# Attention scores straight from the transposed keys, with turned sign and interleaved heads, in a fused attention and two-MoE kernel

## The chip, the cores and the metric

The kernel runs on one core of a Trainium2 chip. The metric is the device time of one execution in microseconds (us). Before the change the median of three runs is 1376.65 us (1376.56 to 1377.2).

The engines are named as the profile names them: PE (TensorE, the matrix engine), PEld (its weight loads), DVE (VectorE), ACT (ScalarE), POOL (GpSimd) and SP (SyncE, which issues nearly all DMAs here). Each runs its own instructions in program order; semaphores tie them together.

## The reference

Block attention over q, k and v (2 batches, 8 heads, 768 positions, 64 wide), then a dense mixture of experts whose gates are balanced by eight Sinkhorn rounds, then a routed mixture of experts. What the change touches is the attention scores:

```
scale = 1/sqrt(64); k_sum = max of k over blocks of 32; v_sum = mean of v over blocks of 32
scores_l = scale * q k^T, kept where |i - j| < 16;   scores_s = scale * q k_sum^T + log(32)
a = softmax over [scores_l, scores_s];   out = a [v ; v_sum]
# dense MoE: P = exp(x w_gate - max); 8 times: divide by row sums, then by column sums
#            out = sum over experts of P[:, e] * relu(x w1[e]) w2[e]
```

## The kernel before, in words

**Attention units.** Attention is cut into 16 units (batch, half of the sequence, pair of heads). The 128 partitions hold two heads of 64 channels each (`par` 0 and 1). A unit has six tiles of 64 queries; each sees a window of 96 key columns and the 24 block maxima `ks`. `transposes_k` (L174) turns the keys into `kT`, a strip of 800 columns, and `transposes_q` (L194) turns the queries into `qT`. `windows` (L203) copies the six overlapping key windows on DVE and the block maxima on ACT into one tile `kTw`, 120 columns per query tile. `scores` (L214) then issues per head six float32 matmuls of 64 by 64 by 120 into one PSUM bank (`sc0` for head 0, `sc1` for head 1), and `hh` picks the upper or lower half of the bank's partitions. `maxima` (L238) adds the mask and takes each row's maximum on DVE, and forms `nb`, minus scale times the maximum, in one small DVE instruction per head. `exponents` (L256) runs six Exp on ACT. `normalise` (L268) divides, with the large multiply on POOL. `flip` (L281) transposes the result on PE, and `apply` (L294) multiplies by the values.

**Order of the work.** `STEPS` (L34) lists these steps, each with the unit that it serves relative to the present one and a cost. The costs say where in the unit's share of time a step's pieces fall; a step that yields in its middle is cut there. `merge` (L835) runs the dense MoE as a sequence of pieces (three large matmuls each) and hands out attention pieces between them: after each piece of the first three MoE units it pulls attention until it has reached `goal`. The first four attention units are done before MoE pieces can be mixed in; short runs of `ones` matmuls (`warm`, L315) are put in there. From MoE unit 3 on, `merge` calls two side tasks between pieces: `token_steps` (36 steps of DVE and ACT work that prepares a Strassen form of the tokens) at every second piece and `gate_steps` (the gate logits and the Sinkhorn rounds, 27 steps) at every third. Whatever is left is run at once at unit 7 or 8. A Sinkhorn round is a `row` step on DVE alone, and a `col` step that begins with a PE product of `ones` and `P` (L934) and goes on with five small DVE instructions.

**PSUM.** In the mixed part, transposes and `apply` share three banks in turn, and `sc0` and `sc1` have one bank each.

Of the kernel before, what the change touches and what calls it, by code (L numbers as in the profile page):

```python
# [19 lines left out]
NEG = -1.0e9  # L20


class Attention:
# [7 lines left out]


    LAG = 2
    STEPS = (  # L34
        ("flip", -LAG, 0.65), ("scores", 0, 1.5), ("windows", 1, 0), ("transposes_q", 1, 0.35),
        ("means", -1, 0.2), ("maxima", 0, 0), ("fill_v", -1, 0), ("exponents", 0, 0),
# [3 lines left out]
    def __init__(self, tc, pool, ident, ones, masks, q, k, v, xhi, xlo, psum):  # L40
# [10 lines left out]
        self.kn, self.qn, self.vw, self.vn, self.sv, self.vs = {}, {}, {}, {}, {}, {}  # L51
        self.kT, self.ks, self.qT, self.kTw = {}, {}, {}, {}
        self.an, self.aT, self.sc = {}, {}, [None, None]
# [140 lines left out]
    def transposes_q(self, b, g, hp):  # L194
        nc = self.nc
        qT = self.pool.tile([128, 384], F32, tag="qT", name="qT", bufs=2)
        qn = self.qn.pop((b, g, hp))
        tr = self.psum("tr", [128, 3, 128])
        self.transpose_rows(tr, qn, 0, self.whole(b, g, hp))
        nc.scalar.copy(qT.rearrange("d (p r) -> d r p", r=3), tr)  # L200
        self.qT[b, g, hp] = qT

    def windows(self, b, g, hp):  # L203
        nc = self.nc
# [7 lines left out]
        self.kTw[b, g, hp] = kTw  # L212

    def scores(self, b, g, hp):  # L214

        nc = self.nc
        qT, kTw = self.qT.pop((b, g, hp)), self.kTw.pop((b, g, hp))
        e = self.pool.tile([128, 2, 3, 120], F32, tag="e", name="e", bufs=self.LAG + 1)
        mx, nb, sm = (
            self.pool.tile([128, 6], F32, tag=n, name=n, bufs=self.LAG + 1) for n in ("mx", "nb", "sm")  # L220
        )
        for par in range(2):
            if par:
                yield
            sc = self.psum(f"sc{par}", [128, 3, 120])
            for j in range(3):
                for hh in range(2):
                    t = 2 * j + hh
                    nc.tensor.matmul(
                        sc[64 * hh:64 * hh + 64, j, :],  # L230
                        qT[64 * par:64 * par + 64, 64 * t:64 * t + 64],
                        kTw[64 * par:64 * par + 64, t, :],
                        start=True, stop=True,
                    )
            self.sc[par] = sc
        self.an[b, g, hp] = e, mx, nb, sm

    def maxima(self, b, g, hp):  # L238
        nc = self.nc
        e, mx, nb, sm = self.an[b, g, hp]  # L240
        for par in range(2):
            sc = self.sc[par]
            for j in range(3):
                qt = 3 * g + j
                m = 0 if qt == 0 else (2 if qt == 5 else 1)
                nc.vector.tensor_tensor_reduce(
                    out=e[:, par, j], in0=sc[:, j], in1=self.masks[:, m], scale=1.0,
                    scalar=-3.0e38, op0=ALU.add, op1=ALU.max,
                    accum_out=mx[:, 3 * par + j:3 * par + j + 1],
                )  # L250
            s = slice(3 * par, 3 * par + 3)
            nc.vector.tensor_scalar(
                out=nb[:, s], in0=mx[:, s], scalar1=-self.scale, scalar2=None, op0=ALU.mult
            )

    def exponents(self, b, g, hp):  # L256
        e, _, nb, sm = self.an[b, g, hp]
        for par in range(2):
            if par:
                yield  # L260
            for j in range(3):
                i = 3 * par + j
                self.nc.scalar.activation(
                    out=e[:, par, j], in_=e[:, par, j], func=ACTF.Exp, scale=self.scale,
                    bias=nb[:, i:i + 1], accum_out=sm[:, i:i + 1],
                )

    def normalise(self, b, g, hp):  # L268
        nc = self.nc
        e, _, _, sm = self.an[b, g, hp]  # L270
        rs = self.pool.tile([128, 6], F32, tag="rs", name="rs", bufs=2)
# [49 lines left out]
    def steps(self, fillers):  # L321
# [22 lines left out]
        for _ in self.transposes_k(*U[0]):  # L344
            yield -LAG
        self.windows(*U[0])
        self.transposes_q(*U[0])
# [32 lines left out]
def make_constants(nc, const, attn):  # L380
# [3 lines left out]
    nc.gpsimd.memset(masks, 0.0)  # L384
    neg = 8.0 * NEG
    for hh in range(2):
# [8 lines left out]
        )  # L395
    nc.gpsimd.memset(masks[:, :, 96:120], 8.0 * LOG_BLOCK)
    nc.gpsimd.memset(masks[0:64, 0, 0:16], neg)
# [437 lines left out]
def merge(attn, moe, sides, late):  # L835
# [4 lines left out]
    for u in moe:  # L840
# [795 lines left out]
def kernel(  # L1636
# [55 lines left out]
    with ExitStack() as stacks:  # L1692
# [186 lines left out]
```

## Time and profile before

| | us |
|---|---|
| median of the three runs | 1376.65 |
| the profiled execution | 1374.23 |
| its span in the trace | 1372.4 |
| PE busy | 1337.4 (97%) |
| DVE busy | 743.5 (54%) |
| ACT busy | 454.3 (33%) |
| POOL busy | 104.6 (8%) |

The profiled execution took 1374.23 us, 1.8 us more than the span from its first to its last instruction, and lies 2.4 us below the median of the other runs. Shares of the span hide that stages have different limits. From the first row on, the stages are: attention alone (to about 50 us), attention mixed with the dense MoE (to about 143 us), the dense MoE with the side tasks (to about 207 us), the dense MoE alone, and the routed MoE from about 1170 us.

### The profile page before, as it was taken

Reading aid. Unit: us, or ns where it says so; the run is one execution under the profiler, and the core shown is the slowest. Engines: PE = TensorE matmul, PEld = TensorE weight load, DVE = VectorE, ACT = ScalarE, POOL = GpSimd, SP = SyncE. Lnnn points to the kernel's source line nnn. Section 1 sums busy time; section 2 is a strip of 40 time slices with the busy share of each in tenths; the row PEclk is TensorE's granted clock in tenths of the full one; section 3 lists DMA queues with packets and bytes.
Section 4 is the critical chain, followed back from the end, with each engine's and each line's share of the span. In section 5 each row is a group of like instructions: output and inputs, shape, how many; then the busy total and the mean of one; then the engine's idle time right before and its main releaser. Section 6 shows DMA issues by size and latency. Waiting matters only on the chain. (4 is left out here: it accounts for less than half of the span.)

```text
span 1372.4 us, 21833 instructions
## 1 busy us (share of the span) xinstructions
PE 1337.4 (97%) x8387; PEld 1176.5 (86%) x8387; DVE 743.5 (54%) x1493; ACT 454.3 (33%) x927; POOL 104.6 (8%) x133
## 2 busy tenths in 40 slices
PE   7999989999999999999999999999999999999996
PEld 7778779998898989989988989899899998788874
DVE  7875594455655555656556555555453347514350
ACT  5866221222323223323223232323221214324451
POOL 5341003200000000000000000000000001111110
PEclk9999999999999999999999999999999999999999
DMA  8742110101101010102011111101021127223440
GB/s 187 160 114 48 32 31 12 51 17 46 32 32 31 32 32 31 54 9 61 10 53 30 33 32 32 31 32 40 23 64 31 60 79 255 69 70 132 154 149 23
DMA packets 90452, 82.71 MB, mean 60 GB/s; under 512 B 44639, under 2 KB 66143, under 8 KB 90336
## 3 DMA queue, kind: packets, MB, share of 16 engines
q1 hardware_dynamic: 87696, 73.34, 18.7%
q0 software_dynamic: 2640, 7.87, 1.7%
q8 instruction: 68, 1.11, 0.4%
q14 instruction: 48, 0.39, 0.1%
HBM read 72.53 MB, written 9.44 MB: 60 GB/s over the span
## 5 line engine op out<-in xcount | busy, mean ns | idle before, releaser
L582 PE MATMUL bank<-hi,hhi 128*128 128x512 f32 x720 | 283.6, 394 | 0.0
L582 PE MATMUL bank<-lo,hhi 128*128 128x512 f32 x720 | 282.8, 393 | 0.0
L582 PE MATMUL bank<-hi,hlo 128*128 128x512 f32 x720 | 282.6, 392 | 0.0
L594 DVE SCALAR_TENSOR_TENSOR acc<-bank,P,acc 128x512 f32<-128x512 f32 x168 | 124.6, 748 | 215.5 <-PE bank L582 215.5
L665 ACT ACTIVATE hhi<-t 128x512 fp32r<-128x512 f32 x144 | 91.3, 634 | 342.9 <-DVE t L691 150.8
L645 PE MATMUL bank<-Thi,hi 128*128 128x256 f32 x576 | 163.3, 283 | 0.0
L645 PE MATMUL bank<-Thi,lo 128*128 128x256 f32 x576 | 163.2, 283 | 0.0
L645 PE MATMUL bank<-Tlo,hi 128*128 128x256 f32 x576 | 162.5, 282 | 0.0
L582 PEld LDWEIGHTS bank<-hi,hlo 128*128 128x128 f32 x720 | 135.4, 188 | 29.2
L582 PEld LDWEIGHTS bank<-hi,hhi 128*128 128x128 f32 x720 | 135.5, 188 | 24.9 <-issue 0.5
L582 PEld LDWEIGHTS bank<-lo,hhi 128*128 128x128 f32 x720 | 135.5, 188 | 23.8
L666 DVE SCALAR_TENSOR_TENSOR hlo<-t,hhi 128x512 fp32r<-128x512 f32 x144 | 99.7, 693 | 100.9 <-ACT hhi L665 100.9
L645 PE MATMUL bank<-xlo,hi 128*128 128x256 f32 x432 | 121.2, 281 | 0.0
L645 PE MATMUL bank<-xhi,hi 128*128 128x256 f32 x432 | 121.2, 281 | 0.0
L645 PE MATMUL bank<-xhi,lo 128*128 128x256 f32 x432 | 121.1, 280 | 0.0
L645 PEld LDWEIGHTS bank<-Thi,hi 128*128 128x128 f32 x576 | 108.8, 189 | 7.9 <-DVE t L690 4.1
L645 PEld LDWEIGHTS bank<-Tlo,hi 128*128 128x128 f32 x576 | 109.0, 189 | 3.8
L645 PEld LDWEIGHTS bank<-Thi,lo 128*128 128x128 f32 x576 | 108.7, 189 | 0.0
L476 DVE TENSOR_TENSOR lo<-raw,hi 128x512 fp32r<-128x512 f32 x120 | 84.3, 716 | 0.6 <-issue 0.3
L645 PEld LDWEIGHTS bank<-xhi,lo 128*128 128x128 f32 x432 | 81.6, 189 | 0.0
L645 PEld LDWEIGHTS bank<-xhi,hi 128*128 128x128 f32 x432 | 81.5, 189 | 0.0
L645 PEld LDWEIGHTS bank<-xlo,hi 128*128 128x128 f32 x432 | 81.5, 189 | 0.0
(287 smaller groups left out, 2203.0 us busy)
## 6 DMA issues: line engine op xcount, KB each, us to landing
raw<-in_moe_w_dram SPq DMA_DIRECT2D x128, 256.0 KB, 2.7
raw<-in_moe_w_dram SPq DMA_DIRECT2D x20, 1024.0 KB, 5.9
kn<-in_k_dram SPq DMA_DIRECT2D x8, 384.0 KB, 4.6
qn<-in_q_dram SPq DMA_DIRECT2D x16, 192.0 KB, 3.9
vn<-in_v_dram SPq DMA_DIRECT2D x8, 384.0 KB, 4.8
x2e<-acc SPq DMA_DIRECT2D x9, 256.0 KB, 2.0
x2d<-acc SPq DMA_DIRECT2D x9, 256.0 KB, 2.3
vw<-in_v_dram SPq DMA_DIRECT2D x16, 96.0 KB, 2.5
```

The costliest lines, as they stand in the source:

```text
L476: self.nc.vector.tensor_tensor(out=lo, in0=src, in1=hi.bitcast(F32), op=ALU.subtract)
L582: nc.tensor.matmul(ps, h, w, start=(n == 0), stop=(n == last))
L594: nc.vector.scalar_tensor_tensor(out=a, in0=ps, scalar=self.P[:, i, e:e + 1], in1=a, op0=ALU.mult, op1=ALU.add)
L645: nc.tensor.matmul(bank[:, 256 * f:256 * f + 256], a[:, o:o + 128], m[:, k], start=first and n == 1, stop=n == 12, skip_group_check=True,)
L665: nc.scalar.activation(out=hi, in_=src, func=ACTF.Relu)
L666: nc.vector.scalar_tensor_tensor(out=lo, in0=src, scalar=0.0, in1=hi.bitcast(F32), op0=ALU.max, op1=ALU.subtract)
```

## The change

The windows are no longer copied: the score matmuls read `kT` and `ks` in place, so each 120-column matmul becomes one of 96 and one of 24 columns. The two heads' matmuls alternate, and all of a unit's scores are issued in one piece. `qT` is scaled by minus the scale when it leaves PSUM; the scores are then negative and scaled, the mask's signs are turned, the row minimum takes the place of the maximum and goes into Exp as its bias, and `nb` falls away. The cost of `scores` in the plan goes from 1.5 to 0.9. In `merge`, attention pieces are pulled two at a time, on every second MoE piece. The side tasks are called at every third and fourth piece.

```diff
-        ("flip", -LAG, 0.65), ("scores", 0, 1.5), ("windows", 1, 0), ("transposes_q", 1, 0.35),
+        ("flip", -LAG, 0.65), ("scores", 0, 0.9), ("transposes_q", 1, 0.35),
...
-        nc.scalar.copy(qT.rearrange("d (p r) -> d r p", r=3), tr)
+        nc.scalar.mul(qT.rearrange("d (p r) -> d r p", r=3), tr, -self.scale)
...
-    def windows(self, b, g, hp):
-        kTw = self.pool.tile([128, 6, 120], F32, tag="kTw", name="kTw", bufs=2)
-        a = self.kT[b, hp][:, 384 * g:800]
-        win = bass.AP(a.tensor, a.offset, [list(a.ap[0]), [64, 6], [1, 96]])
-        nc.vector.tensor_copy(kTw[:, :, 0:96], win)
-        nc.scalar.copy(
-            kTw[:, :, 96:120], self.ks[b, hp].unsqueeze(1).to_broadcast([128, 6, 24])
-        )
...
-        for par in range(2):
-            if par:
-                yield
-            sc = self.psum(f"sc{par}", [128, 3, 120])
-            for j in range(3):
+        self.sc = [self.psum(f"sc{par}", [128, 3, 120]) for par in range(2)]
+        for j in range(3):
+            for own in (False, True):
                 for hh in range(2):
-                    t = 2 * j + hh
-                    nc.tensor.matmul(
-                        sc[64 * hh:64 * hh + 64, j, :],
-                        qT[64 * par:64 * par + 64, 64 * t:64 * t + 64],
-                        kTw[64 * par:64 * par + 64, t, :],
-                        start=True, stop=True,
-                    )
+                    for par in range(2):
+                        t = 2 * j + hh
+                        p = slice(64 * par, 64 * par + 64)
+                        c = 384 * g + 64 * t
+                        nc.tensor.matmul(
+                            self.sc[par][64 * hh:64 * hh + 64, j, slice(96, 120) if own else slice(0, 96)],
+                            qT[p, 64 * t:64 * t + 64],
+                            ks[p] if own else kT[p, c:c + 96],
+                            start=True, stop=True,
+                        )
...
-                    scalar=-3.0e38, op0=ALU.add, op1=ALU.max,
+                    scalar=3.0e38, op0=ALU.add, op1=ALU.min,
...
-            nc.vector.tensor_scalar(
-                out=nb[:, s], in0=mx[:, s], scalar1=-self.scale, scalar2=None, op0=ALU.mult
-            )
...
-                    out=e[:, par, j], in_=e[:, par, j], func=ACTF.Exp, scale=self.scale,
-                    bias=nb[:, i:i + 1], accum_out=sm[:, i:i + 1],
+                    out=e[:, par, j], in_=e[:, par, j], func=ACTF.Exp, scale=-1.0,
+                    bias=mx[:, i:i + 1], accum_out=sm[:, i:i + 1],
...
-            goal += min(4, 4 * (piece + 1) / PIECES[u])
+            goal += min(4, 4 * (piece + 2 - piece % 2) / PIECES[u])
...
-        sides = (token_steps(), 2 * NG - 1, 2, 1), (gate_steps(), 2 * NG, 3, 2)
+        sides = (token_steps(), 2 * NG - 1, 3, 1), (gate_steps(), 2 * NG, 4, 2)
```

PE before, one unit of the mixed part: `ident,e` is `flip`, `kTw,qT` the scores of one head, `xhi`/`xlo` a piece of the MoE, `ident,qn` the query transposes.

```order
L290 MATMUL bank_935<-ident,e 120x128 x3
L290 MATMUL bank_940<-ident,e 120x128 x3
L229 MATMUL bank_949<-kTw,qT 64x120 x6
L562 MATMUL bank_956<-xhi_110,hi_504 128x384
L562 MATMUL bank_956<-xlo_112,hi_504 128x384
L562 MATMUL bank_956<-xhi_110,lo_505 128x384
L229 MATMUL bank_960<-kTw,qT 64x120 x6
L562 MATMUL bank_956<-xhi_110,hi_504 128x384
...
L96 MATMUL bank_974<-ident,qn 128x128 x3
```

PE now at the same place; banks 863 and 864 are the two heads'.

```order
L276 MATMUL bank_850<-ident,e 120x128 x3
L276 MATMUL bank_855<-ident,e 120x128 x3
L220 MATMUL bank_863<-kT_126,qT 64x96
L220 MATMUL bank_864<-kT_126,qT 64x96
...
L220 MATMUL bank_863<-ks,qT 64x24
L220 MATMUL bank_864<-ks,qT 64x24
...
L97 MATMUL bank_890<-ident,qn 128x128 x3
L547 MATMUL bank_897<-xhi_110,hi_407 128x384
L547 MATMUL bank_897<-xlo_112,hi_407 128x384
L547 MATMUL bank_897<-xhi_110,lo_408 128x384
L547 MATMUL bank_897<-xhi_110,hi_407 128x384
```

Two score groups of 6 with a MoE piece behind each have become one group of 24, and two MoE pieces stand together behind it.

DVE before, around the maxima of one unit: `sm` and `rs` end the previous unit's softmax, `kTw` is the window copy of the next unit, ISA is mask and maximum, `kT_124` the key copy two units ahead.

```order
L272 TENSOR_SCALAR sm<-sm 128x6
L273 RECIPROCAL rs<-sm 128x6
L208 COPY kTw<-kT_127 128x6x96
L246 ISA e,mx<-bank_831,masks 128x120
L246 ISA mx 128x1
...
L252 TENSOR_SCALAR nb<-mx 128x3
L246 ISA e,mx<-bank_844,masks 128x120
...
L252 TENSOR_SCALAR nb<-mx 128x3
L185 COPY kT_124<-bank_878 128x3x128
```

DVE now at the same place.

```order
L258 TENSOR_SCALAR sm<-sm 128x6
L259 RECIPROCAL rs<-sm 128x6
L236 ISA e,mx<-bank_863,masks 128x120
L236 ISA mx 128x1
...
L236 ISA e,mx<-bank_864,masks 128x120
...
L186 COPY kT_124<-bank_917 128x3x128
```

The window copy and both `nb` are gone; the rest stands in the same order.

PE before, between two Sinkhorn products: `hi,hhi` and the like are the second MoE matmuls.

```order
L934 MATMUL bank_2317<-P,ones 128x96
L562 MATMUL bank_2305<-xhi_110,hi_2134 128x384
...
L582 MATMUL bank_2329<-hi_510,hhi 128x512
...
L562 MATMUL bank_2351<-xhi_110,hi_2189 128x384
...
L934 MATMUL bank_2357<-P,ones 128x96
```

PE now, between two Sinkhorn products.

```order
L919 MATMUL bank_2513<-P,ones 128x96
L547 MATMUL bank_2505<-xhi_110,hi_2173 128x384
...
L567 MATMUL bank_2529<-hi_2465,hhi 128x512
...
L547 MATMUL bank_2551<-xhi_110,hi_2225 128x384
...
L919 MATMUL bank_2560<-P,ones 128x96
```

Between the two products stood 18 MoE matmuls (six pieces), and now stand 24 (eight pieces). On POOL and on SP the order of instructions is the same before and now.

## Rows read from the trace of the kernel before

**Rows 1.** The page's head.

```profile
span 1372.4 us, 21833 instructions
```

**Rows 2.** Stages: length; busy PE, PEld, DVE, ACT, POOL (count); clock; DMA share, GB/s.

```profile
20.10:50.50 30.40, 27.33 (x327) 24.54 (x327) 25.18 (x85) 25.86 (x83) 15.63 (x17) 0.87 0.79 180
50.50:87.00 36.50, 33.06 (x336) 25.74 (x334) 32.06 (x103) 26.01 (x91) 15.36 (x18) 1.00 0.60 133
87.00:143.00 56.00, 56.00 (x530) 45.64 (x530) 31.16 (x133) 33.82 (x112) 12.98 (x15) 1.00 0.26 64
143.00:207.00 64.00, 58.41 (x290) 47.30 (x289) 50.95 (x129) 18.87 (x37) 0.00 (x0) 0.97 0.12 33
207.00:1170.00 963.00, 962.98 (x5855) 869.30 (x5854) 521.45 (x877) 268.43 (x473) 24.16 (x23) 1.00 0.15 45
```

**Rows 3.** Waits of PE, 0 to 50 us: total us, times, longest.

```profile
PE bank L96 <- DMA qn<-in_q_dram: 4.1, 1, 4.1
PE bank L96 <- DVE sm L272: 1.2, 1, 1.2
PE bank L96 <- DVE lo L476: 1.2, 1, 1.2
```

**Rows 4.** Waits of PE, 50 to 240 us.

```profile
PE bank L934 <- DVE P L929: 3.8, 5, 2.0
PE bank L290 <- DVE kT L185: 3.1, 4, 1.8
PE bank L913 <- DVE lg_max L911: 1.5, 1, 1.5
```

**Rows 5.** Timeline of PE in the mixed part: start, length, instruction.

```profile
58.10 0.44 PE L562 MATMUL bank<-xhi,hi 128*128 128x384 f32 x1
58.38 0.34 PE L562 MATMUL bank<-xlo,hi 128*128 128x384 f32 x1
58.55 0.33 PE L562 MATMUL bank<-xhi,lo 128*128 128x384 f32 x1
58.82 0.83 PE L229 MATMUL bank<-kTw,qT 64*64 64x120 f32 x12
59.58 0.44 PE L562 MATMUL bank<-xhi,hi 128*128 128x384 f32 x1
```

**Rows 6.** Timeline of PE in attention alone.

```profile
25.94 1.10 PE L229 MATMUL bank<-kTw,qT 64*64 64x120 f32 x24
26.97 0.55 PE L96 MATMUL bank<-ident,qn 128*128 128x128 f32 x3
...
27.67 0.92 PE L303 MATMUL bank<-aT,vw 120*64 120x64 f32 x24
28.52 2.05 PE L319 MATMUL bank<-ones 128*128 128x128 f32 x16
```

**Rows 7.** Groups on DVE, 0 to 130 us: busy us, mean ns, idle before.

```profile
L246 DVE CUSTOM_DVE_ANT_0 e<-bank,masks 128x120 f32<-128x120 f32 x96 | 21.7, 274 | 0.8 <-PE bank L229 0.8
L208 DVE COPY kTw<-kT 128x576 f32<-128x576 f32 x16 | 14.9, 929 | 0.0
L252 DVE TENSOR_SCALAR nb<-mx 128x3 f32<-128x3 f32 x32 | 8.6, 268 | 1.1
```

**Rows 8.** Timeline of DVE and POOL around two window copies.

```profile
52.86 0.42 DVE L208 COPY kTw<-kT 128x576 f32<-128x576 f32 x1
...
76.21 1.64 DVE L208 COPY kTw<-kT 128x576 f32<-128x576 f32 x1
...
76.01 1.39 POOL L275 TENSOR_TENSOR e<-e,rs 128x720 f32<-128x720 f32 x1 [4.47 <-DVE rs L273]
```

**Rows 9.** Groups on DVE, 55.26 to 79.73 us (three units).

```profile
L208 DVE COPY kTw<-kT 128x576 f32<-128x576 f32 x3 | 3.9, 1294 | 0.0
```

**Rows 10.** Part of the Sinkhorn stretch; columns as in Rows 2.

```profile
169.00:191.67 22.67, 19.56 (x97) 16.51 (x98) 19.90 (x56) 6.91 (x13) 0.00 (x0) 1.00 0.12 38
191.67:195.08 3.41, 3.41 (x11) 2.93 (x11) 3.27 (x10) 1.00 (x2) 0.00 (x0) 0.50 0.43 134
```

More of the change, by code (lines that the diff above doesn't have):

```diff
@@ L51, in __init__ @@
         self.kn, self.qn, self.vw, self.vn, self.sv, self.vs = {}, {}, {}, {}, {}, {}
-        self.kT, self.ks, self.qT, self.kTw = {}, {}, {}, {}
+        self.kT, self.ks, self.qT = {}, {}, {}
         self.an, self.aT, self.sc = {}, {}, [None, None]
@@ L214, in scores @@
     def scores(self, b, g, hp):
         nc = self.nc
-        qT, kTw = self.qT.pop((b, g, hp)), self.kTw.pop((b, g, hp))
+        qT, kT, ks = self.qT.pop((b, g, hp)), self.kT[b, hp], self.ks[b, hp]
         e = self.pool.tile([128, 2, 3, 120], F32, tag="e", name="e", bufs=self.LAG + 1)
-        mx, nb, sm = (
-            self.pool.tile([128, 6], F32, tag=n, name=n, bufs=self.LAG + 1) for n in ("mx", "nb", "sm")
-        )
-        for par in range(2):
-            if par:
-                yield
-            sc = self.psum(f"sc{par}", [128, 3, 120])
-            for j in range(3):
-                for hh in range(2):
-                    t = 2 * j + hh
-                    nc.tensor.matmul(
-                        sc[64 * hh:64 * hh + 64, j, :],
-                        qT[64 * par:64 * par + 64, 64 * t:64 * t + 64],
-                        kTw[64 * par:64 * par + 64, t, :],
-                        start=True, stop=True,
-                    )
-            self.sc[par] = sc
@@ L236, in scores @@
-        self.an[b, g, hp] = e, mx, nb, sm
+        mx, sm = (
+            self.pool.tile([128, 6], F32, tag=n, name=n, bufs=self.LAG + 1) for n in ("mx", "sm")
+        )
+        self.sc = [self.psum(f"sc{par}", [128, 3, 120]) for par in range(2)]
+        for j in range(3):
+            for own in (False, True):
+                for hh in range(2):
+                    for par in range(2):
[8 more added lines that the diff above has]
+                        )
@@ L238, in maxima @@
+        self.an[b, g, hp] = e, mx, sm
     def maxima(self, b, g, hp):
         nc = self.nc
-        e, mx, nb, sm = self.an[b, g, hp]
+        e, mx, sm = self.an[b, g, hp]
         for par in range(2):
@@ L247, in maxima @@
                     out=e[:, par, j], in0=sc[:, j], in1=self.masks[:, m], scale=1.0,
-                    scalar=-3.0e38, op0=ALU.add, op1=ALU.max,
+                    scalar=3.0e38, op0=ALU.add, op1=ALU.min,
                     accum_out=mx[:, 3 * par + j:3 * par + j + 1],
                 )
-            s = slice(3 * par, 3 * par + 3)
-            nc.vector.tensor_scalar(
-                out=nb[:, s], in0=mx[:, s], scalar1=-self.scale, scalar2=None, op0=ALU.mult
-            )
     def exponents(self, b, g, hp):
-        e, _, nb, sm = self.an[b, g, hp]
+        e, mx, sm = self.an[b, g, hp]
         for par in range(2):
@@ L269, in normalise @@
         nc = self.nc
-        e, _, _, sm = self.an[b, g, hp]
+        e, _, sm = self.an[b, g, hp]
         rs = self.pool.tile([128, 6], F32, tag="rs", name="rs", bufs=2)
@@ L345, in steps @@
             yield -LAG
-        self.windows(*U[0])
         self.transposes_q(*U[0])
@@ L384, in make_constants @@
     nc.gpsimd.memset(masks, 0.0)
-    neg = 8.0 * NEG
+    neg = -NEG
     for hh in range(2):
@@ L395, in make_constants @@
         )
-    nc.gpsimd.memset(masks[:, :, 96:120], 8.0 * LOG_BLOCK)
+    nc.gpsimd.memset(masks[:, :, 96:120], -LOG_BLOCK)
     nc.gpsimd.memset(masks[0:64, 0, 0:16], neg)
```

2 lines of the change are left out of this document (removed).

## The prediction

> **What bounds the kernel now.** I read the stages first. In the trace the span is 1372.4 us [rows 1]; PE is busy in nearly all of it, and from 207 to 1170 us it has no gap at all [rows 2]. Nothing there is touched, so what is won before 207 us arrives at the end, unless a stage before it gives it back. Before 207 us four stages differ. In attention alone (20.1 to 50.5 us) PE, DVE and ACT each have idle time and PE's clock is down for part of it: no engine is full, and transfers and waits set the pace. From 50.5 to 87 us PE is busy 33.06 and DVE 32.06 of 36.5 us, two engines nearly full. From 87 to 143 us PE alone is full. From 143 to 207 us PE has gaps while DVE is busy 50.95 of 64 us [rows 2]. Then I read who ended PE's waits: in attention alone query rows that come late by DMA, 4.1 us, and two waits of 1.2 us put down to DVE [rows 3]; later only DVE, 3.1 us for a bank of transposed keys that is not yet copied out, and 3.8 and 1.5 us for the Sinkhorn steps [rows 4]. PE work and DVE lateness are the two prices to set.
>
> **Part 1: the scores on PE, where they are mixed with MoE pieces.** One head's scores take 0.76 us from their start to the next MoE matmul (58.82 to 59.58). Around them a border is paid: the MoE matmul before them lasts 0.27 us (58.55 to 58.82) instead of 0.17 (58.38 to 58.55), and the first one after such a group 0.28 (58.10 to 58.38) instead of 0.17 [rows 5]. One insertion costs 0.76 + 0.10 + 0.11 = 0.97 us, a unit of two heads 1.94.
>
> Now there is one insertion of 24 matmuls. A float32 matmul streams its columns four times in all, and the upper and lower half of a bank run side by side: six matmuls of 120 columns at 2.4 GHz (the granted clock is 1.00 in this stage, rows 2) are six slots of 2 x 2 x 120 / 2.4 = 0.2 us of passes, two matmuls at a time, so 6 x 0.10 = 0.60 us, and the 0.16 us left of 0.76 is start and end. A 96-column slot is then 0.080 us. A 24-column slot would be 0.020 by streaming alone; the nearest row is the 64-column product of the values: 24 records, 12 slots, from 27.67 to 28.52, so (0.85 - 0.16) / 12 = 0.058 us [rows 6]. I take 0.058. The bounds are 0.020 and 0.100 (as long as a 120-column slot).
>
> That two heads run at the same time is shown where both stand next to each other: 25.94 to 26.97 is 1.03 us [rows 6], while 0.16 + 12 x 0.10 = 1.36 would be one after the other. They overlap by 0.33 although the second head is queued behind all of the first. With the heads alternating I take full overlap: 0.16 + 6 x 0.080 + 6 x 0.058 = 0.99 us, with borders 1.20, so a unit saves 0.74 us. The 24-column bounds make it 0.97 and 0.49. No overlap at all gives 0.16 + 12 x 0.138 = 1.82, with borders 2.03, a loss of 0.09 us.
>
> The trace has 230 score records from 50.5 to 143 us, about 19 insertions of 12, or 9.5 units. So 9.5 x 0.74 = **7.0 us**, between -0.9 and 9.2.
>
> The Trainium skill (TensorEngine Tiling, Instruction Overhead) says that each matmul has some 60 cycles of overhead, so that one column costs as much as sixty; this speaks against cutting 120 into 96 and 24. By it a 24-column slot costs what 60 columns do, 0.050 us, and the saving would be 7.5 us; streaming alone would make it 9.2. No run here has shown 24 columns; the 64-column row above is near the rule.
>
> **Part 2: DVE in the mixed part.** Per unit one window copy (0.929 us mean) and two `nb` (0.268 each) go: 1.47 us [rows 7]. In three units from 55.26 to 79.73 us the copies alone take 3.9 us [rows 9]. The stretch from 50.5 to 87 us holds nearly five units: DVE falls from 32.06 to about 25.5, PE from 33.06 to about 29.7 (4.5 x 0.74). PE is then the fuller engine by 4 us, so most of its 3.1 us of waits for the key copies [rows 4] should go. I take **2.3 us**, between 0 and 3.1. ACT loses its copy of the block maxima and is not near full.
>
> The copy's length is not its own: it takes 0.42 us with POOL quiet and 1.64 while POOL's normalising multiply runs (76.01 for 1.39 us) [rows 8]. So one may ask whether the wait merely passes on to the next DVE instruction. What follows it now is the masked minimum out of PSUM, and the masked maxima of before, the same instruction, averaged 274 ns over all 96, POOL busy or not [rows 7]: nothing passes on there.
>
> The Trainium skill (SBUF — State Buffer, SBUF: two separate sides) says that DVE and GpSimd share a port pair as an exclusive lock, which blocks a DVE instruction with two SBUF inputs or in a two-port mode for the whole of the other's instruction. By that rule the wait could pass to the splits of the weights (two SBUF inputs) a little further on. Then only the bare 0.42 of the copy is sure, part 2 shrinks to about 1 us, and the sum by 1.3.
>
> **Part 3: attention alone.** The same DVE and PE work goes there, but the wait of 4.1 us is for query rows on their way, and SP issues the same DMAs in the same order. The two waits of 1.2 us are met by the same instruction, the query transposes, which also wait for their rows; I count them as transfers. Exp can start on its first sixth instead of its first half. I take **0.8 us**; the bounds are -0.5 (a transfer in a new collision) and 3.3 (both waits and 0.9 of ACT's).
>
> **Part 4: the side tasks.** Sinkhorn waits are 3.8 + 1.5 = 5.3 us [rows 4], and after the longest the clock is at half (0.50) for 3.41 us [rows 10], which costs 1.7 us of PE work. PE did nothing for 2.0 us just before that. Together 7.0 us. Now 24 MoE matmuls stand between two products where 18 stood, so the time in which DVE can finish the `col` and `row` chains grows by a third, and the token steps come at two thirds of the rate. From 169 to 191.67 us DVE was busy 19.90 of 22.67 us [rows 10]; with a third more PE work under it (19.56 x 4/3 = 26), it would be busy about 76%. Some stays: the maximum of the logits is reduced and transposed within one step, so PE still meets DVE's backlog there, and four weight splits fall in a bunch somewhere. I leave 1.7 us standing and take **5.3 us**, between 2.5 and 7.0. The clock's loss should go with the long gap. The steps need 36 calls at 9 per unit and 27 at 7 per unit, so both end within units 3 to 6, before they would be run in a bunch at units 7 and 8; that costs nothing.
>
> Two MoE pieces now stand together, which saves some borders against transposes; there the border is small, and I leave it out.
>
> **The sum.** 7.0 + 2.3 + 0.8 + 5.3 = 15.4 us. The profiled execution took 1374.23 us, so it would take 1358.8; the median of the runs lies 2.4 us above it, and 1376.65 - 15.4 = **1361.3 us**.
>
> **Rivals.** *Less is won, because transfers or DVE keep the mixed part's pace* (about 1366). Half of the waits before 87 us are for rows, and a unit there needs seven or eight DMAs, issued one after another by SP. If from 50.5 to 87 us the pace stays, part 2 and half of part 1 (4.5 x 0.74 = 3.3) go, with part 3: 15.4 - 2.3 - 3.3 - 0.8 = 9.0, or 1367.7; if only the port rule holds or the heads overlap by half, 1363 to 1366. Against it: DVE, not DMA, ended every wait after 50 us [rows 4].
>
> *More is won* (about 1355). Short slots cost 0.020 (9.2), the key waits go entirely (3.1), attention alone gives 2.5 and Sinkhorn 6.8: 21.6, so 1355. For it: every stage loses DVE work. Against it: each term would have to be at its good end.
>
> *Slower: changing the row half costs a drain.* The border of about 0.10 us [rows 5] is paid when PE goes between the full array and half of it. If PE paid the like at each of the 23 changes of head within a unit, the scores would take 0.99 + 2.3 us; over 9.5 units that is 22 us more than forecast and in attention alone, where 6.5 units run, some 12 more beyond the slack: 1361.3 + 34 = 1395. It decides from 15.4 / (16 x 23) = 0.042 us per change on. Against it: the overlap of two neighbouring heads, 1.03 against 1.36 us [rows 6].
>
> *No gain:* the heads run one after the other (part 1 at -0.9) and the Sinkhorn waits stay because DVE is still late there: 2.3 + 0.8 + 0.5 - 0.9 = 2.7, so 1374. Against it: rows 6 again, and the third more of cover.
>
> **Chances.** Forecast (1358 to 1364.5) 0.55, less won 0.23, more won 0.14, slower 0.04, no gain 0.04. A run of this kernel cannot tell less than 0.2%, 2.75 us, from no change; so faster 0.92, same 0.04, slower 0.04. The range from 1354.5 to 1369 holds the forecast, nearly all of "less" and about half of "more".
>
> **What would show it.** Right: in the mixed part one group of score records per unit, about 1.0 us from its start to the next instruction, the two heads' records side by side; no window copies; key-copy waits under 1 us; Sinkhorn waits under 2 us and the clock at 1.00 from 169 to 210 us; from there to the end the same length as before. Wrong: score groups of 1.8 us or more; PE waiting for query or key rows between 50 and 87 us; Sinkhorn waits of 4 us or more, or a side task run in a bunch at unit 7; a tail after 1150 us that is longer than before.

## The result

| | median, us | runs, us | ratio to before, 95% interval |
|---|---|---|---|
| before | 1376.61 | 1375.1 to 1377.2 (4) | |
| the changed kernel | 1359.69 | 1358.83 to 1360.33 (4) | 0.9878, 0.9861 to 0.9896 |

The forecast was 1361.3 us, with a range of 1354.5 to 1369.0. The median fell by 16.9 us where 15.4 were expected. Its profiled execution took 1360.04 us against 1374.23, so the profiles account for 14.2.

### The profile page after: what moved, and what is told of

Its sections match the earlier page's. It is cut to its first block, busy times and chain, and to the rows that moved or that the text cites. A ratio compares the mean times of both kernels' runs of the same rounds, so it can differ in the third digit from the quotient of the medians.

```text
span 1358.3 us, 22536 instructions
## 1 busy us (share of the span) xinstructions
PE 1324.5 (98%) x8771; PEld 1174.7 (86%) x8771; DVE 721.7 (53%) x1445; ACT 449.9 (33%) x911; POOL 103.2 (8%) x133
```

## The profile after

The head of the page, to set against [rows 1]:

```profile
span 1358.3 us, 22536 instructions
```

To see where the 14.1 us of span come from, both traces are cut at the same work, not at the same time. The landmarks are the starts of the 1st, 13th and 29th relu that ACT takes from the dense MoE's banks (`hhi` out of `bank`), and the last relu of the routed MoE. The kernel before, columns as in [rows 2]:

```profile
0.00:57.67 57.67, 47.98 (x554) 42.55 (x556) 44.66 (x148) 38.74 (x128) 25.80 (x52) 0.91 0.78 173
57.67:145.74 88.07, 85.10 (x813) 68.28 (x810) 58.53 (x212) 53.18 (x175) 26.73 (x30) 1.00 0.37 85
145.74:230.09 84.35, 78.77 (x392) 66.46 (x391) 57.50 (x146) 20.86 (x42) 9.38 (x6) 0.98 0.09 26
230.09:1347.03 1116.94, 1113.11 (x6578) 989.45 (x6576) 581.53 (x986) 338.60 (x580) 40.73 (x43) 1.00 0.18 56
```

The changed kernel:

```profile
0.00:58.04 58.04, 44.65 (x712) 41.22 (x713) 33.50 (x126) 37.10 (x121) 24.60 (x52) 0.91 0.76 176
58.04:136.88 78.84, 78.25 (x1037) 68.60 (x1036) 46.93 (x185) 51.41 (x167) 25.69 (x30) 1.00 0.40 92
136.88:214.32 77.44, 75.90 (x393) 65.64 (x392) 57.78 (x147) 20.58 (x41) 4.25 (x3) 1.00 0.09 28
214.32:1332.96 1118.64, 1113.22 (x6578) 989.47 (x6576) 582.22 (x986) 337.88 (x580) 46.71 (x47) 1.00 0.17 56
```

Read the lengths line by line. Up to the first relu nothing is won (0.4 us lost), although DVE works 11 us less and PE 3.3 us less there. The mixed part is 9.2 us shorter, the side stretch 6.9, and the rest 1.7 longer. That last loss cannot be put down to the change: no line of that stretch was touched, and in the 14 traces shown here it lasts 1116.9 to 1119.6 us.

Who ended PE's waits, from 0 to 50 us (to set against [rows 3]):

```profile
PE bank L97 <- DMA qn<-in_q_dram: 6.8, 2, 5.4
PE bank L97 <- DVE mx L236: 1.4, 1, 1.4
```

And from 50 to 250 us (against [rows 4]):

```profile
PE bank L97 <- DMA qn<-in_q_dram: 3.4, 1, 3.4
PE bank L919 <- DVE P L914: 1.1, 1, 1.1
PE bank L898 <- DVE lg_max L896: 0.5, 1, 0.5
```

The waits for the key copies (3.1 us) are gone and the Sinkhorn waits fell from 5.3 to 1.6. But query rows, 4.1 us before, now cost 10.2, and one such wait has moved behind 50 us, where there was none. The timeline of PE shows it, and a window over the stretch behind it shows the clock:

```profile
52.27 0.87 PE L97 MATMUL bank<-ident,qn 128*128 128x128 f32 x3 [3.38 <-DMA qn<-in_q_dram]
```

```profile
52.27:58.00 5.73, 5.72 (x47) 5.36 (x48) 2.34 (x3) 4.41 (x15) 0.28 (x2) 0.73 0.78 160
```

The transposes of a later unit's queries wait 3.4 us ahead of the very first MoE piece, and PE goes on at a granted clock of 0.73 (a mean of stretches at its two levels, 0.5 and 1).

One unit's scores on PE (to set against [rows 5]):

```profile
58.59 0.40 PE L220 MATMUL bank<-kT,qT 64*64 64x96 f32 x8
58.80 0.26 PE L220 MATMUL bank<-ks,qT 64*64 64x24 f32 x8
58.89 0.38 PE L220 MATMUL bank<-kT,qT 64*64 64x96 f32 x8
59.08 0.26 PE L220 MATMUL bank<-ks,qT 64*64 64x24 f32 x8
59.17 0.38 PE L220 MATMUL bank<-kT,qT 64*64 64x96 f32 x8
59.37 0.26 PE L220 MATMUL bank<-ks,qT 64*64 64x24 f32 x8
59.56 0.55 PE L97 MATMUL bank<-ident,qn 128*128 128x128 f32 x3
```

58.59 to 59.56 is 0.97 us for both heads; one head alone took 0.76.

On DVE the masked minimum and the weight splits, 0 to 130 us (against [rows 7]):

```profile
L236 DVE CUSTOM_DVE_ANT_0 e<-bank,masks 128x120 f32<-128x120 f32 x96 | 20.6, 277 | 1.6 <-PE bank L220 1.6
L461 DVE TENSOR_TENSOR lo<-raw,hi 128x512 fp32r<-128x512 f32 x8 | 7.6, 970 | 0.5 <-ACT hi L460 0.3
```

and the same splits in the kernel before:

```profile
L476 DVE TENSOR_TENSOR lo<-raw,hi 128x512 fp32r<-128x512 f32 x8 | 8.9, 1128 | 0.5 <-issue 0.3
```

Neither inherited the window copy's long waits: the minimum kept its length (277 ns after, 274 before) and the splits became shorter. That they became shorter is not the missing copy's doing: in the two kernels below that copy again they take 986 and 988 ns.

## The experiments

Each ratio is to runs of the kernel before on the same chip; the first row has the medians of these runs, and the landmarks of the one trace of that kernel. The stages are set side by side at the landmarks above, with the 5th relu added. Between the 5th and the 13th every kernel here has the same MoE matmuls and five units of scores; between the 1st and the 5th, three to four units.

Each kernel has one trace, so it matters how far two traces of the same work differ. Two pairs show it. Up to the 13th relu "side steps alone" runs the same instructions as the kernel before, and "new scores, old pacing" the same as "one piece at a time"; their edits come into force only later. From the 5th to the 13th relu the traces of a pair agree within 0.01 us. The first relu differs by 0.1 us in one pair and by 2.4 in the other. From the 1st to the 5th one pair takes 21.29 us twice, and the other 28.28 and 30.28, where the longer one ran in part at the lower clock:

```profile
57.67:85.95 28.28, 25.31 (x263) 19.82 (x260) 25.31 (x77) 17.84 (x60) 12.78 (x15) 1.00 0.60 135
57.53:87.81 30.28, 27.85 (x261) 22.37 (x258) 25.33 (x77) 17.82 (x61) 13.51 (x16) 0.89 0.59 126
```

So 2.4 us at the first relu, and 2 us in a stretch with waits, can be luck; a few tenths from the 5th to the 13th are not.

| kernel | median, us | ratio to before, 95% interval | 1st relu | 5th | 13th | 29th |
|---|---|---|---|---|---|---|
| before | 1375.96 to 1377.12 | | 57.67 | 85.95 | 145.74 | 230.09 |
| changed | 1359.69 | 0.9878, 0.9861 to 0.9896 | 58.04 | 80.60 | 136.88 | 214.32 |
| side steps alone | 1369.46 | 0.9956, 0.9938 to 0.9974 | 57.53 | 87.81 | 147.60 | 225.02 |
| new scores, old pacing | 1365.09 | 0.9921, 0.9902 to 0.9939 | 58.15 | 79.44 | 135.14 | 219.47 |
| one piece at a time | 1357.33 | 0.9867, 0.9846 to 0.9889 | 55.79 | 77.08 | 132.77 | 210.22 |
| pairs later | 1363.25 | 0.9910, 0.9893 to 0.9927 | 52.83 | 81.99 | 138.51 | 215.99 |
| heads apart | 1364.79 | 0.9914, 0.9901 to 0.9928 | 59.57 | 84.12 | 143.34 | 220.81 |
| wide block maxima | 1364.55 | 0.9912, 0.9895 to 0.9928 | 57.11 | 82.47 | 143.25 | 220.69 |
| copies read | 1356.63 | 0.9854, 0.9837 to 0.9871 | 56.33 | 80.14 | 134.88 | 212.32 |
| copies idle | 1358.81 | 0.9866, 0.9852 to 0.9880 | 59.08 | 83.89 | 139.56 | 217.00 |
| alternation alone | 1368.36 | 0.9937, 0.9924 to 0.9949 | 57.42 | 84.74 | 139.82 | 224.12 |
| value rows later | 1355.46 | 0.9854, 0.9836 to 0.9872 | 54.17 | 75.47 | 131.17 | 208.63 |
| copies for six units | 1352.88 | 0.9826, 0.9814 to 0.9839 | 55.23 | 77.73 | 132.48 | 209.94 |
| value rows by POOL | 1358.47 | 0.9867, 0.9852 to 0.9881 | 53.73 | 74.75 | 130.45 | 207.88 |

### Which part gave what

**Side steps alone.** The kernel before with one line changed.

```diff
-        sides = (token_steps(), 2 * NG - 1, 2, 1), (gate_steps(), 2 * NG, 3, 2)
+        sides = (token_steps(), 2 * NG - 1, 3, 1), (gate_steps(), 2 * NG, 4, 2)
```

> The kernel before with only the side steps spaced as in the changed kernel (every third and fourth MoE piece). Theory: the 7.0 us that the changed kernel gained between the 13th and the 29th relu of the dense MoE (146 to 213 us in the kernel before) come from the spacing alone: 1376.6 - 7.0 = 1369.6 us, with no change before 143 us and Sinkhorn waits of 2 us or less. Rival: the lighter attention work is what freed DVE at the head of that stretch, and the spacing alone gains 4 us or less: 1372.6 us or more, with Sinkhorn waits of 3 us or more left.

Measured: 6.5 us less. From the 13th to the 29th relu it takes 77.42 us (the changed kernel 77.44, before 84.35), and its Sinkhorn waits are those of the changed kernel:

```profile
PE bank L934 <- DVE P L929: 1.1, 1, 1.1
PE bank L913 <- DVE lg_max L911: 0.5, 1, 0.5
```

The gain of that stretch is the spacing's, and independent of the scores.

**New scores, old pacing.** The changed kernel with the goal and the side steps of before.

```diff
-            goal += min(4, 4 * (piece + 2 - piece % 2) / PIECES[u])
+            goal += min(4, 4 * (piece + 1) / PIECES[u])
...
-        sides = (token_steps(), 2 * NG - 1, 3, 1), (gate_steps(), 2 * NG, 4, 2)
+        sides = (token_steps(), 2 * NG - 1, 2, 1), (gate_steps(), 2 * NG, 3, 2)
```

> The new attention (scores in place, heads alternating, turned sign) with the old pacing: one attention piece at a time, side steps at every second and third MoE piece. Theory: the mixed part gains its 9.2 us as in the changed kernel, and the first stages another 2 to 4 because the query transposes no longer run half a unit ahead of their rows; the side stretch gains nothing: 1376.6 - 9.2 - 3 = 1364.4 us, between 1362 and 1368. Rival: standing MoE pieces together (fewer borders) is a good part of the gain of the mixed part: 1370 us or more.

Measured: 10.9 us less, within the theory's range. From the 5th relu to the 13th it takes 55.70 us (changed kernel 56.28, before 59.79): pulling in pairs gave nothing to the mixed part and cost it 0.6 us. The saving expected ahead of it did not come: the first relu is at 58.15, and query rows still cost 7.3 and 2.7 us. The total was met because the mixed part gave more, 11.1 us from the first relu to the 13th instead of 9.2.

**One piece at a time.** The changed kernel with the goal alone set back.

```diff
-            goal += min(4, 4 * (piece + 2 - piece % 2) / PIECES[u])
+            goal += min(4, 4 * (piece + 1) / PIECES[u])
```

> The changed kernel with attention pulled one piece at a time again. Theory: two at a time cost more than they gave: the first pull comes before the first MoE piece and now holds the query transposes of the unit after next, so PE waits 3.4 us for their rows and then runs at half clock; without it 1359.7 - 2 to 5 = 1355 to 1358 us, and the wait after 48 us is under 1 us. Rival: transfers set the pace, the wait comes back one transpose later: 1359 to 1361 us. Second rival: two at a time saves borders between MoE pieces and attention worth more than the wait: over 1361 us.

Measured: 1357.33 us, in the theory's range, though its interval and the changed kernel's overlap widely. The trace agrees in one half and not in the other. The wait stays, at 2.8 us:

```profile
PE bank L97 <- DMA qn<-in_q_dram: 2.8, 1, 2.8
```

But PE's clock is up behind it:

```profile
50.50:87.00 36.50, 36.14 (x546) 32.49 (x547) 27.95 (x102) 29.44 (x96) 18.66 (x24) 1.00 0.74 162
```

What two pieces at a time cost is shown for one part only, 0.6 us from the 5th relu to the 13th: 56.28 against 55.69 to 55.70 in the four kernels that have the same scores and pull one. The other two parts, 0.6 us of this wait and 5.73 x 0.27 = 1.5 of the clock, are an estimate from these rows. With the same instructions "new scores, old pacing" reached its first relu 2.4 us later, and "copies idle" below, which also pulls one piece at a time, has a clock of 0.95 from 50.5 to 87 us, as the changed kernel has. The three parts make 2.7, and the medians differ by 2.4.

**Pairs later.** The pull comes behind two MoE pieces.

```diff
-            goal += min(4, 4 * (piece + 2 - piece % 2) / PIECES[u])
+            goal += min(4, 4 * (piece - piece % 2) / PIECES[u])
```

> The changed kernel with the two attention pieces pulled after two MoE pieces instead of ahead of them (the whole attention half a unit later against the MoE). Theory: the first two MoE pieces (some 2 us) run while the query rows are on their way, the wait of 3.4 us shrinks to 1 us or less and the half clock behind it (0.73 in 52.3 to 58 us) goes: 1359.7 - 4 = 1355.7 us, between 1354 and 1358. Rival: the rows are the pace, the wait stays in sum: 1359 to 1361 us.

A miss: 1363.25 us. The first relu comes 5.2 us sooner, since MoE pieces run before the wait, and the query wait behind 50 us is still 2.4 us. But the stretch to the 5th relu grows from 22.6 to 29.2: it holds the attention work that was put behind, and waits for banks that the changed kernel has next to none of (0.3 us):

```profile
PE bank L97 <- PE bank L220: 1.7, 3, 0.6
PE bank L276 <- DVE kT L186: 1.6, 4, 0.5
```

At the 13th relu 1.6 us are lost; the medians differ by 3.6, and the traces do not explain the rest.

Filling a wait with work that is due anyway gains only if what was put behind does not wait in its turn.

### What made the scores cheaper

**Heads apart.** The changed kernel with `par` as the outermost loop.

```diff
-        for j in range(3):
-            for own in (False, True):
-                for hh in range(2):
-                    for par in range(2):
+        for par in range(2):
+            for j in range(3):
+                for own in (False, True):
+                    for hh in range(2):
```

> The changed kernel with all of head 0's 12 score matmuls ahead of head 1's 12, still in place and in one piece. Theory: the heads overlap in full only where they alternate; one behind the other they overlap by the 0.33 us of the kernel before [rows 6], so a group takes about 1.49 us instead of the 0.97 measured when alternating; 0.5 us in each of the 9 units of the mixed part, where PE is full: 1359.7 + 4.7 = 1364.4 us, between 1362 and 1367. Rival: the order of the heads is indifferent, since matmuls of different row halves run beside each other wherever they are queued: a group of 1.0 us, 1359 to 1360.5 us.

Measured: 1364.79 us, the theory's number. The group on PE:

```profile
60.12 0.38 PE L220 MATMUL bank<-kT,qT 64*64 64x96 f32 x4
60.33 0.25 PE L220 MATMUL bank<-ks,qT 64*64 64x24 f32 x4
...
60.70 0.40 PE L220 MATMUL bank<-kT,qT 64*64 64x96 f32 x8
60.89 0.28 PE L220 MATMUL bank<-ks,qT 64*64 64x24 f32 x8
...
61.67 0.55 PE L97 MATMUL bank<-ident,qn 128*128 128x128 f32 x3
```

1.55 us instead of 0.97. The heads run side by side (8 records to a row instead of 4) only in the one place where the last third of head 0 meets the first of head 1. The Trainium skill (TensorE: Matmul & The Clock Gate, Part 3: Packing small matmuls) says that matmuls on different tiles of the array overlap but keep the order of the queue. On the overlap the trace agrees. On the order it does not: the row at 60.70 already holds head 1's first four 96-column records, ahead of the row at 60.89 with head 0's last 24-column ones, which the kernel issues before them.

**Copies read.** One piece at a time, scores again from copied windows in 12 matmuls of 120 columns, heads alternating (`windows` as in the kernel before).

```diff
-        ("flip", -LAG, 0.65), ("scores", 0, 0.9), ("transposes_q", 1, 0.35),
+        ("flip", -LAG, 0.65), ("scores", 0, 0.9), ("windows", 1, 0), ("transposes_q", 1, 0.35),
...
-                            ks[p] if own else kT[p, c:c + 96],
...
+                        kTw[p, t, :],
```

> The new attention pulled one piece at a time, but the scores read copied windows again (12 matmuls of 120 columns in a unit, heads alternating; the two copies are back on DVE and ACT). It tells what reading in place gave beside the alternation. Theory: on PE the copies are worth something, a group of 3 x 0.24 + 0.1 = 0.84 instead of 0.97 us, 1.2 us over the mixed part; on DVE they cost 0.93 us a unit, which comes back as waits for the key copies where DVE is nearly full (50 to 87 us), up to 2.5 us: 1357.3 + 1 = 1358.3, between 1356 and 1360. Rival: DVE was no bound there, and the copies win: 1356 us. Second rival: the port shared by DVE and POOL makes the copies dear and 3 us or more are lost: over 1360 us.

```profile
55.77 0.84 PE L229 MATMUL bank<-kTw,qT 64*64 64x120 f32 x24
56.55 0.44 PE L557 MATMUL bank<-xhi,hi 128*128 128x384 f32 x1
```

Both heads take 0.78 us, against 0.76 for one before: alternating, the second head costs almost nothing, and reading in place costs PE 0.19 us a unit. In time this kernel and "one piece at a time" are alike (0.9854 and 0.9867, intervals overlapping). That is the balance that the theory expected, though 1356.63 lies nearer to the first rival's 1356 than to its 1358.3. By stages the copies lose 2.5 us from the 1st relu to the 5th (23.81 against 21.29) and win 0.95 from there to the 13th (54.74 against 55.69).

**Copies idle.** One piece at a time, with the copies made (`windows` as in the kernel before) and read by nobody; the scores read `kT` and `ks` in place.

```diff
-        ("flip", -LAG, 0.65), ("scores", 0, 0.9), ("transposes_q", 1, 0.35),
+        ("flip", -LAG, 0.65), ("scores", 0, 0.9), ("windows", 1, 0), ("transposes_q", 1, 0.35),
```

> The new attention pulled one piece at a time (1357.3 us), with the two window copies put back on DVE and ACT but read by nobody: PE's work is as without them. It prices DVE's relief alone. Theory: the copies cost where DVE is nearly full, between the first and the fifth relu of the dense MoE, and nothing later; the forecast's term was 2.3 us, the kernel that reads the copies lost 2.5 us in that stretch although its PE work is lighter by 0.19 us a unit, so 3 us: 1357.3 + 3 = 1360.3, between 1359 and 1361.5. Rival: DVE has room there, and the loss of the copy-reading kernel came from its later start: 1357 to 1358.5 us.

The median, 1358.81 us, lies between the two expectations, and the total cannot tell them apart: the ratio is 0.9866, and 0.9867 without the copies. What the copies cost can only be read from the stages. Without copies, from the first relu to the 5th and on to the 13th:

```profile
55.79:77.08 21.29, 21.29 (x348) 19.50 (x340) 18.34 (x66) 17.77 (x59) 11.63 (x14) 1.00 0.77 164
77.08:132.77 55.69, 55.69 (x669) 47.53 (x668) 27.26 (x117) 33.50 (x110) 14.09 (x16) 1.00 0.29 69
```

With idle copies:

```profile
59.08:83.89 24.81, 23.39 (x370) 20.04 (x368) 24.16 (x71) 18.61 (x63) 12.45 (x15) 1.00 0.67 142
83.89:139.56 55.67, 55.67 (x669) 47.53 (x668) 29.39 (x122) 34.37 (x115) 14.29 (x16) 1.00 0.29 68
```

In the first stretch DVE is busy 24.16 of 24.81 us and PE waits. It is 3.5 us longer. About 0.9 of that is other work: 28 score records (of 48 to a unit, 0.97 us) and 3 transposes fall behind the first relu here and ahead of it in the other kernel. That leaves 2.6. The changed kernel, which pulls in pairs but has the same score records in this stretch, takes 22.56, or 2.25 us less. Half of the 2.25 is PE's idle time (1.42 against 0.28), the other half longer busy time for the same records, which is not explained. Of the 5.6 us that the four copies take on DVE there, less than half thus shows. In the second stretch PE has no gap either way, and the copies cost nothing.

These are single traces, and of unlike executions: here the slowest of four was profiled (1361.03 us), there the fastest (1355.01). But the stretch repeats. The four kernels that pull one piece at a time, with the changed kernel's scores and no copies, take 21.02 to 21.30 us in it; the two that copy for every unit take 23.81 and 24.81.

**Alternation alone.** The kernel before with the heads' matmuls alternating.

```diff
-        for par in range(2):
-            if par:
-                yield
-            sc = self.psum(f"sc{par}", [128, 3, 120])
-            for j in range(3):
-                for hh in range(2):
+        self.sc = [self.psum(f"sc{par}", [128, 3, 120]) for par in range(2)]
+        for j in range(3):
+            for hh in range(2):
+                for par in range(2):
...
```

> The kernel before, with one edit: the two heads' 120-column score matmuls alternate, in one piece (copies, maxima with two small instructions, pacing and side steps as before). Theory: the alternation is what gives PE its gain, a group of 0.78 us instead of two of 0.76 with three borders, about 1.0 us a unit over 9 units; DVE, still with its copies, takes back a good part between 50 and 87 us, where it was busy 32 of 36.5 us [rows 2]: a gain of 5 to 8 us, 1370 us. Rival: without the copies' removal DVE takes back all of the early part and PE's gain is 4 us or less: 1372.6 us or more.

Measured: 8.8 us less, just beyond the theory's 5 to 8; the profiled executions differ by 5.6. Its two stretches, to the 5th relu and to the 13th:

```profile
57.42:84.74 27.32, 23.05 (x264) 18.76 (x254) 25.30 (x77) 17.89 (x60) 11.82 (x13) 0.94 0.63 136
84.74:139.82 55.08, 55.08 (x552) 45.82 (x551) 33.13 (x135) 35.03 (x115) 14.89 (x18) 1.00 0.28 68
```

Before, they took 28.28 and 59.79 us, in the changed kernel 22.56 and 56.28. Where PE alone is full, alternating saves 4.7 us, more than the changed kernel's 3.5. In the first stretch only 1.0 us is left, much as the rival had it: PE's idle time grows from 3.0 to 4.3 us beside a DVE busy 25.30 of 27.32, the key waits from 3.1 to 4.5, and the clock of 0.94 takes a part too.

**Wide block maxima.** One piece at a time; the 24 columns for 128 queries in one matmul.

```diff
-                            self.sc[par][64 * hh:64 * hh + 64, j, slice(96, 120) if own else slice(0, 96)],
-                            qT[p, 64 * t:64 * t + 64],
-                            ks[p] if own else kT[p, c:c + 96],
...
+                    self.sc[par][:, j, 96:120],
+                    qT[p, 128 * j:128 * j + 128],
+                    ks[p],
```

> The new attention pulled one piece at a time (as in the fastest run so far, 1357.3 us), with the block-maxima product done for 128 queries at once: six matmuls of 128 stationary columns and 24 moving ones for a unit instead of twelve of 64 and 24. Theory: the 24-column slot of 0.09 us is set by the number of instructions (four matmuls in it), not by its columns; half as many make it about 0.05, so a group falls from 0.97 to 0.85 us and the time by 9 x 0.12 = 1.1 us. Rival: going between half and full columns of the array costs a border of up to 0.10 us each way; three such changes of shape make the group 1.2 us or more and the time 2 us longer.

The rival won, at more than its price: 1364.55 us, 7.2 above "one piece at a time" where it said 2.

```profile
56.58 0.40 PE L219 MATMUL bank<-kT,qT 64*64 64x96 f32 x8
56.90 0.41 PE L227 MATMUL bank<-ks,qT 64*128 64x24 f32 x4
57.24 0.40 PE L219 MATMUL bank<-kT,qT 64*64 64x96 f32 x8
```

With half the instructions a 24-column step lasts 0.34 us instead of 0.09, and the 96-column step beside it 0.32 instead of 0.20. The group takes 1.98 us.

### Towards a faster kernel

**Value rows later.** One piece at a time, value rows loaded a unit later.

```diff
         load(self.load_v, 0)
-        load(self.load_v, 1)
...
-            load(self.load_v, i + 2)
+            load(self.load_v, i + 1)
```

> The new attention pulled one piece at a time, with each unit's value rows loaded one unit later, so that SP issues five DMAs (0.6 us each) less ahead of the third unit's query rows and every later one. Theory: PE's waits for query rows (6.7 us before 50 us, 2.8 at 48 to 51) come from SP, which issues without a break and reaches the query DMA late; 3 us of them go: 1357.3 - 3 = 1354.3 us, between 1353 and 1356. Rival: the DMA engines are the pace (share 0.7 to 0.9 there), the rows land no earlier, or value rows now come late: 1357 us or more.

1355.46 us, within the theory's range, 1.9 below "one piece at a time", with intervals that overlap. What was moved is the queue: in the kernel with one piece at a time SP issues nearly without a pause up to 20 us, and the third unit's query rows stand behind ten value DMAs, of which the first row here is the last:

```profile
12.54 0.61 SPq L163 DMA_DIRECT2D vw<-in_v_dram  x1
13.24 0.62 SPq L70 DMA_DIRECT2D kn<-in_k_dram  x1
13.96 0.80 SPq L70 DMA_DIRECT2D qn<-in_q_dram  x1
```

With the value rows moved no PE wait for rows is left after 50 us, but before it there are still four, 7.7 us; together it was 9.5.

**Copies for six units.** The same, with copied windows for the last six units.

```diff
     def windows(self, b, g, hp):
+        if not (b and (g or hp >= 2)):
+            return
```

> The fastest run so far (one piece at a time, value rows one unit later, 1355.5 us), with copied windows for the last six units alone, where DVE has room. Theory: a score group takes 0.78 us with copies and 0.97 without; 6 x 0.19 = 1.2 us less in the stretch where PE alone is full: 1354.3 us, between 1353.5 and 1355. Rival: the copies come back as DVE waits there too: 1355.5 us or more.

1352.88 us, the lowest median of all and below the theory's range: 24 us below the kernel before, 7 below the changed one. The stretch from the 5th relu to the 13th is 0.95 us shorter (54.75 against 55.70), which is the theory's mechanism. The rest of the 2.6 us between this median and the last is not explained: the intervals of the two ratios still touch, and the profiled executions took 1354.25 and 1353.99 us.

**Value rows by POOL.** As "value rows later", with two of each unit's value DMAs issued by POOL.

```diff
-            nc.sync.dma_start(
+            (nc.gpsimd if h else nc.sync).dma_start(
```

> The same kernel (1355.5 us), with head 1's two value DMAs of each unit issued by POOL instead of SP. Theory: SP's issuing is the pace of attention alone, about 0.6 us for each of seven or eight DMAs a unit; with two fewer, query rows are asked for sooner and PE's 7.7 us of waits for them before 50 us fall to 5 or less: 1353.5 us, between 1351.5 and 1354.5. Rival: POOL, busy half of that stretch, pays over 1 us for each and its normalising multiply comes late, or the DMA engines are the pace: 1356 us or more.

A miss in its total, 1358.47 us, but not for the rival's reason: the query waits fell to 5.4 us, PE's wait for the normalising multiply is 0.2 us as it was, and the 29th relu comes 0.75 us sooner. It is lost at the very end, below.

## Why the prediction was right

**Scores on PE (7.0 us) and DVE (2.3).** Together 9.3, measured 9.2 from the first relu to the 13th; against the other trace of the same instructions, "side steps alone", it would be 11.2. The group was put at 0.99 us and takes 0.97. A unit was to save 0.74 us where PE is full: from the 5th relu to the 13th five units save 3.5, 0.70 each (0.82 with one piece at a time). DVE's relief was put at 2.3 between 50 and 87 us: the idle copies cost 2.25 to 2.6. What the two terms hide is that they do not add freely: without DVE's relief PE's saving in the first stretch was 1.0 us (alternation alone, at a clock of 0.94) where it came to 5.7 with it.

**The 24-column slot.** A third of a group, four matmuls of 96 and four of 24 columns, was put at 0.160 + 0.116 us and takes about 0.195 + 0.09 from start to start: the short slots were put too long, the long ones too short, and the sum held. By the Trainium skill (TensorEngine Tiling, Instruction Overhead) one column costs what sixty do, so that a 24-column slot was 0.050 us by the prediction's estimate; cutting a unit's six slots in two then costs 6 x (0.080 + 0.050 - 0.100) = 0.18 us. The trace agrees: the two groups, 0.97 and 0.78 us, are 0.19 apart, and the 0.058 us that the prediction took instead makes it 0.23.

**Where the gain really is.** The prediction followed the change in treating the reading in place as its centre. The runs put it elsewhere: with the heads alternating, in place or copied makes no difference that the medians can tell. By the stages in place is right while DVE is full, copied afterwards, and the kernel that does each in its part has the lowest median.

**Attention alone (0.8 us).** This step failed: up to the first relu the trace shows 0.4 us lost (with the 2.4 us of scatter above, nothing that can be told from zero). The prediction held that "SP issues the same DMAs in the same order", and so counted the wait for rows as unchanged; but the same arrivals are met by a PE that asks sooner. The runs bear this out: the longer the score group, the less PE waits for query rows. With pairs, groups of 0.97 and 1.55 us go with waits of 10.2 and 6.3 us in all; with one piece at a time, 0.97 and 1.98 us with 9.5 and 3.1. What PE saves there it spends waiting. The prediction also left out what two pieces at a time do to the first pull, which now holds the query transposes ahead of the first MoE piece: 3.4 us of wait and a clock of 0.73 behind it. With one piece at a time 2.8 us of the wait stay, so the pairs made little of it. The bounds, -0.5 to 3.3, did hold the term. But one of the prediction's own signs of being wrong came, PE waiting for query rows behind 50 us, and with it went its argument that DVE and not DMA ends every wait there.

**Side tasks (5.3 us).** The mechanism was right and the term too small: 6.9 us. PE's idle time there fell by 4.0 us (5.58 to 1.54), as forecast within 0.4; its busy time for the same instructions fell by 2.9, of which 1.7 is the half clock [rows 10]. The other 1.2 us were not assigned; fewer interruptions of the stream of matmuls are a candidate, not a finding. That the spacing alone does it is shown: "side steps alone" has the changed kernel's 77.4 us, and "new scores, old pacing" the 84.3 of before.

**The step from profile to median.** The profiles differ by 14.2 us, the medians by 16.9. The forecast carried over the 2.4 us by which the profiled execution of before lay under its median; the changed kernel's lies 0.35 above. Two small errors of opposite sign, 1.2 us too much in the sum and 2.7 too little here, made the number look better than its steps: that it came within 1.6 us is in part luck.

**Rivals.** "Slower", a drain at each change of head, is refuted by the 0.97 us. Another change does cost something like it: going between 64 and 128 stationary columns (wide block maxima). "Less is won" had its mechanism, rows that come late, in attention alone and not in the mixed part, where no wait for rows stands behind the first relu. The wait that might have passed from the window copy to the splits of the weights did not: they take 970 ns without the copy and 986 with it idle.

## What to carry to other kernels

Here small matmuls on different parts of the array ran side by side only where they stood close together in the program (0.97 us against 1.55), so alternate them and keep their shapes alike; that was worth more than avoiding the copy. The copy was free where PE alone was full and showed in the time where DVE was full too, so decide stage by stage and not for the kernel as a whole. Before reading a stage of one trace against a stage of another, look for two traces of the same instructions: they tell what is luck. When work is regrouped, look at the first group: it may put a wait ahead of work that used to cover it.

## What was not expected of the hardware

**The last stationary shape matters.** Alternating 64 by 64 with 64 by 128 tiles lifts a group from 0.97 to 1.98 us with fewer instructions. That the change of shape is the cause, and not the wide matmul by itself, is a reading: the unchanged 96-column step beside it grew too, but no run has the wide ones without the alternation.

**DMAs issued by POOL cost at the end of the program.** The last scatter of "value rows later", and its span:

```profile
span 1352.3 us, 22548 instructions
```

```profile
1342.35 0.98 POOL L1563 DMA_INDIRECT out_dram<-o,r_idxf  x1 [6.85 <-ACTq L1610]
```

The same with 32 more DMAs on POOL, all of them long finished:

```profile
span 1356.8 us, 22577 instructions
```

```profile
1340.93 0.98 POOL L1563 DMA_INDIRECT out_dram<-o,r_idxf  x1 [6.74 <-ACTq L1610]
```

From the start of the last scatter to the end of the span it takes 15.8 us instead of 9.9. In the trace POOL's closing drain lasts 5.38 us instead of 2.77, and each of the five semaphore steps ahead of it 1.44 instead of 0.80. All 13 other traces have 2.77 and 0.80, and 33 DMAs on POOL where this one has 65: the drain is 84 and 83 ns for each. Without the 5.9 us the median would lie in the theory's range. That the count of DMAs sets the length is a reading of one kernel against 13; it was not tested by itself.
